# Seven-product sums made inside one PSUM bank, and the second product three steps behind instead of two

## The chip, the cores and the metric

One core of a Trainium2 chip runs the whole program. The metric is the device time of one execution in microseconds, as the median of several runs without the profiler. Engines are named as in the profile: PE is TensorE's matmuls, PEld its weight loads, DVE is VectorE, ACT is ScalarE, POOL is GpSimd, SP is SyncE, whose queue issues nearly all DMAs (SPq in the views).

## The reference

Two blocks follow each other. The first is a chunked state-space scan over 4 sequences of 8 heads, 768 positions, head size 32 and state size 16. The second is a feed-forward block on its output, read as 3072 tokens of 256 numbers:

```python
def _moe_ref(x, w_in, w_out) -> np.ndarray:
    h = x @ w_in              # 3072x256 by 256x2048
    g = h * np.cos(h)
    return (g @ w_out).astype(np.float32)   # 2048x256
```

All is float32. The scan yields, for every chunk of 32 positions, a masked product within the chunk and a product with the running state; the state decays and takes up the chunk.

## The kernel before

**Blocks and steps.** The 768 positions are cut into six blocks of 128 (`c` = 0 to 5), each with all four sequences, so that a block has 512 tokens. The scan of a block gives `yT[c]`, the features of its tokens with the feature index on the partitions. The feed-forward block then runs in steps `n` = 16 c + f. In block 0 a step takes one of two halves of the tokens (`u` = f % 2) and 256 columns of the hidden layer (`j` = f // 2); in later blocks `u` = f // 8 and `j` = f % 8. So a unit (c, u) of 256 tokens is summed over eight steps.

**One step.** `first(n)` makes `hp[n]`, 256 hidden columns by 256 tokens, in one PSUM bank (512 numbers a partition): four matmuls 128x256, eight records in the trace. Then `wind_k(n)` on ACT rounds hp/2pi to a whole number `k`, `wind_w(n)` on DVE takes the rest `w`, `gate(n)` on ACT makes the cosine, and `gated(n)` on DVE multiplies it with hp into `gT[n]`, which frees the bank. `second(n)` multiplies gT with `w_out` and adds to the unit's sums `o`. In the loop, `second(n - LAG)` stands behind `first(n)` on PE; LAG is 2.

**Seven products for eight.** From block 1 on, `seven(n)` makes the second product by Strassen's scheme in Winograd's form: a 2x2 block product in seven 128x128x128 products (14 records) in place of eight. `differ(n)` on POOL makes four differences `gd[n]` of the blocks of gT (three instructions; a ring of three buffers), `differ_w` those of the weights. The seven sums of a unit stay in two banks, `lo` and `hi`. After the unit's last step ACT copies them to `ps`, DVE or POOL adds them up into `sum`, and SP stores that. In block 0 the copy is called `ob`.

**Seven products in the first product too.** The steps in `runs` (f = 10 to 12 of blocks 2 to 4, and the thirteen steps 81 to 93) make `hp` by the same scheme in `first7`. Product 1 goes to quarter 0 of the hp bank, products 6, 7, 5 and 4 to two more banks (`at6`, `at`, from a pair called m), 3 and 2 to hp. ACT copies quarter 0 to SBUF (`parts`), and DVE makes four sums (lines 773, 776, 778 and 781). `first_of_seven(n)` writes the order out by hand: products 1 and 6 of step n, the copy, `wind_k(n - 1)`, the other five products, then `wind_w(n - 1)`, the sums, `gate(n - 1)` and `gated(n - 1)`; the seven products of `second(n - LAG)` follow on PE in one piece.

**Banks.** PSUM has eight: two of tag h (hp), two of tag o (the sums), and two pairs of tag scan. In the runs hp takes turns between the two of tag h and one half of a pair, so a step's hp bank was that of step n - 3; outside the runs hp has the two of tag h, and `first(n)` waits for `gated(n - 2)`.

**Order of work.** The order on every engine is the order in which the code issues; a wait stops all that stands behind it on its engine. At the start, `first_steps` sets out steps 0 to 3, between which DVE, ACT and POOL unpack the weights (`grade`, `join`; each 512 KB piece of `w_in` and `w_out` comes as 8-byte words). The loop starts at n = 4 (`AHEAD`), where no `second` stands:

```python
        if n == AHEAD + 1:
            second(AHEAD - LAG)
        if n >= LAG and n != AHEAD:
            second(n - LAG)
```

The scan of block 2 and later works on `blocks`, loaded by SP in groups of two issues (`load_blocks`, lines 147 and 150), transposed by DVE (line 582), scaled by ACT to `cT` (line 591), and multiplied on PE by `inner2` (line 603), for block 2 behind the `second` of step 24.

Of the kernel before, what the change touches and what calls it, by code (L numbers as in the profile page):

```python
# [10 lines left out]
I32 = mybir.dt.int32  # L11
AF = mybir.ActivationFunctionType
ALU = mybir.AluOpType
# [12 lines left out]
def kernel(  # L26
# [23 lines left out]
    HH = H // 2  # L50
    RB = 96
    NU = NB * H * NC // RB
    LAG = 2
    W = P // 2

    const = ctx.enter_context(tc.tile_pool(name="const", bufs=1))
# [606 lines left out]
                between()  # L663

    def wind_k(n):
        k = ffn.tile([P, TB], I32, tag="k", name="k")
        ACT.activation(k, hp[n], AF.Copy, bias=0.25, scale=INV_2PI)  # L667
        turns[n] = k

# [47 lines left out]


    win4 = w_in.rearrange("p k (j e f) -> p k j e f", j=NJ, e=2)
    wid, yd = [], {}  # L720

    def differ_in(i, js):

# [18 lines left out]
        eng.tensor_tensor(out=d[:, i, us], in0=a_, in1=b_,  # L742
                          op=ALU.add if i in (1, 2) else ALU.subtract)

    def first7(n, to_, at6, at, between):

        c, f = divmod(n, NF)
        u, j = turn_of(n)
        hp[n] = to_
        to_ = to_.rearrange("p (q m) -> p q m", q=4)  # L750
        w = {1: win4[:, 0, j, 0], 2: win4[:, 1, j, 0], 3: wid[3][:, j], 4: win4[:, 1, j, 1],
             5: wid[0][:, j], 6: wid[2][:, j], 7: wid[1][:, j]}
        d, y = yd[c][:, :, u], yT[c][:, u].rearrange("p k (h i) -> p k h i", h=2)
        y_ = {1: y[:, 0, 0], 2: y[:, 1, 0], 3: y[:, 1, 1], 4: d[:, 3], 5: d[:, 0], 6: d[:, 2],
              7: d[:, 1]}
        dst = {6: at6, 1: to_[:, 0], 7: at[:, 0], 5: at[:, 1], 4: at[:, 2], 3: to_[:, 1],
               2: to_[:, 0]}

        def product(q):
            PE.matmul(dst[q], lhsT=w[q], rhs=y_[q], start=(q in (6, 1, 7)), stop=True,  # L760
                      skip_group_check=True)

        parts = ms[3].rearrange("p (t q m) -> p t q m", t=2, q=4)[:, n % 2]
        add = dict(op=ALU.add)
        for q in (1, 6):
            product(q)
        ACT.copy(out=parts[:, 0], in_=to_[:, 0])
        between()
        while finished:
            finished.pop()()  # L770
        for q in (7, 5, 4, 3, 2):
            product(q)
        V.tensor_tensor(out=parts[:, 1], in0=at6, in1=parts[:, 0], **add)

        def rest():
            V.tensor_tensor(out=parts[:, 2:4], in0=at[:, 0:2],
                            in1=parts[:, 1:2].to_broadcast([P, 2, P]), **add)
            V.tensor_tensor(out=to_[:, 2:4], in0=at[:, 2:0:-1],
                            in1=parts[:, 2:3].to_broadcast([P, 2, P]), **add)

        return rest, lambda: V.tensor_tensor(out=to_[:, 1], in0=to_[:, 1], in1=parts[:, 3], **add)

    unit_rows = out.rearrange("(s q k i) m -> q k i s m", s=2, q=2, i=W)

    def second(n):
        c, f = divmod(n, NF)
        if c > 0:
            seven(n)
            return
        u, j = turn_of(n)  # L790
        if j == 0:
            o[c, u] = bank([P, 2, DM], "o", "o")
        g = gT.pop(n)
        for e in range(2):
            for t in range(2):
                PE.matmul(o[c, u][:, t], lhsT=g[:, 2 * e + t], rhs=w_out[:, 2 * j + e],  # L796
                          start=(j == e == t == 0), stop=(j == NJ - 1 and e == 1),
                          skip_group_check=True)
        if j < NJ - 1:
            return  # L800
        ob = conv.tile([P, 2, DM], FP32, tag="last", bufs=3, name="ob")
        ACT.copy(out=ob, in_=o[c, u])
        for p in range(2):
            nc.sync.dma_start(out=unit_rows[p, u], in_=ob[p * W:(p + 1) * W])

    def seven(n):

        c = n // NF
        u, j = turn_of(n)
        final = n >= NC * NF - NJ  # L810
        if j == 0:


            if final:
                t = pair("o").rearrange("p b (q m) -> p b q m", m=P)
                mid, hi = t[:, 0], t[:, 1]
                lo = bank([P, 4, P], "o", "o")
                o[c, u] = (mid, lo, hi, {1: mid[:, 0], 6: mid[:, 1], 7: mid[:, 2], 5: mid[:, 3],
                                         2: lo[:, 0], 3: lo[:, 1], 4: hi[:, 0]})
            else:  # L820
                lo, hi = (bank([P, 4, P], "o", "o") for _ in range(2))
                o[c, u] = (lo, hi, {1: lo[:, 0], 6: lo[:, 1], 2: lo[:, 2], 7: hi[:, 0],
                                    5: hi[:, 1], 4: hi[:, 2], 3: hi[:, 3]})
        at = o[c, u][-1]
        g = gT.pop(n)
        if n == NC * NF - 1:
            last_step(g, *o[c, u][1:3])
            return
        d = gd.pop(n)
        w = {1: w4[:, j, 0, 0], 2: w4[:, j, 1, 0], 3: w4[:, j, 1, 1], 4: wd[3][:, j],  # L830
             5: wd[0][:, j], 6: wd[2][:, j], 7: wd[1][:, j]}
        a_ = {1: g[:, 0], 2: g[:, 2], 3: d[:, 3], 4: g[:, 3], 5: d[:, 0], 6: d[:, 2], 7: d[:, 1]}
        starts = (1, 2, 4) if final else (1, 7)
        for q in ((1, 4, 7, 5, 6, 2, 3) if final else (1, 2, 7, 5, 6, 4, 3) if n in sevens else
                  (1, 2, 6, 7, 5, 4, 3)):
            PE.matmul(at[q], lhsT=a_[q], rhs=w[q], start=(j == 0 and q in starts),  # L836
                      stop=(j == NJ - 1), skip_group_check=True)
        if final and j == NJ - 2:
            shared(o[c, u][0])
        if j < NJ - 1:  # L840
            return

        sum_ = two.tile([P, 7, P], FP32, tag="sum", bufs=1, name="sum")
        ps = two.tile([P, 7, P], FP32, tag="ps", bufs=1, name="ps")
        lo, hi = o[c, u][0:2]

        def take():
            ACT.copy(out=ps[:, 0:3], in_=lo[:, 0:3])
            ACT.copy(out=ps[:, 3:7], in_=hi)

        if n + LAG + 1 in sevens:
            finished.append(take)
        else:
            take()

        def rest(of=range(4), eng=V):
            for dst, a_, b_ in [((sum_[:, 0:2], ps[:, 1:3], ps[:, 0:1]),
                                 (sum_[:, 5:7], ps[:, 3:5], sum_[:, 0:1]),
                                 (sum_[:, 3:5], ps[:, 5:3:-1], sum_[:, 5:6]),
                                 (sum_[:, 2:3], ps[:, 6:7], sum_[:, 6:7]))[i] for i in of]:  # L860
                eng.tensor_tensor(out=dst, in0=a_, in1=b_.to_broadcast([P, dst.shape[1], P]),
                                  op=ALU.add)
            for s in range(2 if 3 in of else 0):
                nc.sync.dma_start(out=unit_rows[s, 2 * c + u], in_=sum_[s * W:(s + 1) * W, 1:5].rearrange(
                                      "p (t h) m -> p t (h m)", t=2))

        unsummed.append(rest)
# [156 lines left out]
    runs = [*(range(NF * c + 10, NF * c + 13) for c in range(2, NC - 1)),  # L1024
            range(NC * NF - 15, NC * NF - 2)]
    sevens = {n: r for r in runs for n in r}
    late, at_ = [], {}

    def first_of_seven(n):

        i = n - sevens.get(n, sevens.get(n - 1))[0]
        if i == 0:
            at_["hp"] = pair("hp")[:, 0]
            at_["m"] = pair("m").rearrange("p b (q m) -> p b q m", m=P)
        if n == NC * NF - NJ + LAG + 1:
            at_["hp"] = bank([P, TB], "hp", "o")
        to_ = at_["hp"] if i % 3 == 1 else bank([P, TB], "hp", "h")
        if n not in sevens:
            first(n, to_=to_)
            return  # L1040
        sums, last_sum = first7(n, to_, at_["m"][:, 1, 0], at_["m"][:, 0],
                                lambda: wind_k(n - 1) if i else None)
        if i:
            wind_w(late[0])
        sums()
        gate(late[0]) if i else None
        gated(late.pop())
        last_sum()

    def first_steps():  # L1050

# [52 lines left out]
    for n in range(AHEAD, NC * NF + LAG):  # L1104
        c, f = divmod(n, NF)
        if n < NC * NF:
# [10 lines left out]
                load_along(2, (2 * (n == NF), 2 * (n == NF) + 1))  # L1117
            for e, i in chunks_at(n, "along"):
                load_along(e + 1, (2 * i, 2 * i + 1))
            if n in sevens or n - 1 in sevens:  # L1120
                first_of_seven(n)
            else:
                first(n)
            if n not in sevens and n - 1 in sevens:
                wind(n - 1)
                gate(n - 1)
                gated(late.pop())
            closing = f == NF - 1 and 1 <= c < NC - 1
            take_y = finish2(c + 1) if closing else None
            if n not in sevens:  # L1130
# [29 lines left out]
            behind = [lambda k=k: weights(k, 1) for k in units_at(n - 1, 3)] + behind  # L1160
            if not joins and behind:
                behind.pop(0)()
            if n + 1 in sevens or n in sevens:
                late.append(n)
            else:
                gated(n)
            if closing:
                take_y(1)
# [28 lines left out]
        for start, js in zip((2 * NF - 5, 3 * NF - 3, 4 * NF - 3),  # L1197
                             (slice(2, 5), slice(0, 2), slice(5, NJ))):
            if start <= n < start + 4:
                differ_in(n - start, js)  # L1200
        if n == AHEAD + 1:
            second(AHEAD - LAG)
        if n >= LAG and n != AHEAD:
            second(n - LAG)
        for e, _ in chunks_at(n, "inner"):
            inner2(e)
        for k in units_at(n, 3):
# [49 lines left out]
```

## Time and profile before

| | us |
|---|---|
| median of 3 runs | 364.75 (364.12 to 365.27) |
| profiled execution: span from first to last instruction (the page gives no other time of it) | 369.8 |
| PE busy | 359.4 |
| PEld busy | 327.8 |
| DVE busy | 270.8 |
| POOL busy | 233.0 |
| ACT busy | 182.3 |

| group | count | mean ns of one |
|---|---|---|
| PE hp, 128x256 (line 660) | 592 | 386 |
| PE 128x128 products (lines 760, 836) | 308 and 1106 | 275 to 278 |
| ACT k, line 667 | 96 | 595 |
| ACT cosine, line 682 | 96 | 723 |
| DVE w, line 673 | 96 | 685 |
| DVE gT, line 687 | 96 | 682 |
| DVE sums of hp, lines 773, 776, 778, 781 | 22 each | 291, 415, 433, 289 |
| ACT copy of quarter 0, line 767 | 22 | 262 |
| ACT copies `lo`, `hi`, lines 848, 849 | 9 each | 471, 596 |
| ACT copy 128x256 (yT, line 636) | 16 | 379 |

A record's duration contains time in which the next one already runs, so that matmuls are costed by the distance between starts: 0.112 us for a 128x128 record and 0.216 for a 128x256 one in this trace. A float32 matmul leaves two records. The span lies above the median, so that the profiled execution is slower than the others; differences are worked out within the profile.

### The profile page before, as it was taken

How to read it: one execution, taken by the hardware profiler on the slowest of the kernel's cores; microseconds unless marked ns; L12 is line 12 of the kernel's file. 1: busy time of each engine (PE TensorE's matmuls, PEld its weight loads, DVE VectorE, ACT ScalarE, POOL GpSimd, SP SyncE). 2: the span in 40 equal slices, each digit the busy share in tenths (PEclk: the TensorE clock that was granted, in tenths of full speed). 3: DMA queues.
4: the chain of work that ended last, by engine and by line, in shares of the span. 5: the costliest groups of instructions: out<-in, count | busy, mean ns of one | idle time of the engine just before them, and what ended most of it. 6: DMA issues, size and time to landing. Idle time of an engine off the chain costs nothing.

```text
span 369.8 us, 10169 instructions
## 1 busy us (share of the span) xinstructions
PE 359.4 (97%) x4034; PEld 327.8 (89%) x4034; DVE 270.8 (73%) x492; ACT 182.3 (49%) x346; POOL 233.0 (63%) x375
## 2 busy tenths in 40 slices
PE   8999999999959999999999999999999999999995
PEld 5688888898948989999999999999999999999995
DVE  7699988588735794887757788756796565688874
ACT  4588756463433435453545453445553444455542
POOL 6567656679816676466676656679556465375572
PEclk9999999999996999999999999999999999999999
DMA  7996855593566416344005441001010001001002
GB/s 141 259 361 133 186 119 92 82 151 64 125 100 90 88 44 98 52 79 82 13 4 110 59 79 37 6 4 42 2 30 0 2 2 31 2 2 29 2 10 51
DMA packets 97328, 26.43 MB, mean 71 GB/s; under 512 B 87328, under 2 KB 93184, under 8 KB 97280
## 3 DMA queue, kind: packets, MB, share of 16 engines
q1 hardware_dynamic: 96032, 25.38, 33.7%
q8 instruction: 32, 0.52, 0.6%
q10 hardware_dynamic: 1248, 0.39, 0.5%
q14 instruction: 16, 0.13, 0.1%
HBM read 22.36 MB, written 3.34 MB: 69 GB/s over the span
## 4 chain that ended last, share of the span: by engine, by line
PE 83%; DVE 4%; POOL 3%; ACT 2%; DMA 2%; SPq 2%; issue 2%; DVEq 0%; ACTq 0%; POOLq 0%
PE o L836 31%; PE hp L660 30%; PE m L760 5%; PE o L796 5%; PE hp L760 4%; PE y L629 2%; PE g L603 1%; DMA blocks<-in_C_dram 1%; SPq L150 1%; POOL gd L712 1%; DVE mag L261 1%; DMA bc<-in_B_dram 1%; POOL gd L714 1%; DVE w L673 1%; PE y L617 1%
## 5 line engine op out<-in xcount | busy, mean ns | idle before, releaser
L660 PE MATMUL hp<-yT,w_in 128*128 128x256 f32 x592 | 143.0, 386 | 0.4 <-DVE gT L687 0.4
L660 PEld LDWEIGHTS hp<-yT,w_in 128*128 128x128 f32 x592 | 108.8, 192 | 15.6 <-issue 1.6
L712 POOL TENSOR_TENSOR gd<-gT 128x256 f32<-128x256 f32 x79 | 59.8, 758 | 89.4 <-DVE gT L687 74.3
L682 ACT ACTIVATE w<-w,quarter 128x512 f32<-128x512 f32 x96 | 69.4, 723 | 68.1 <-DVE w L673 68.0
L673 DVE SCALAR_TENSOR_TENSOR w<-hp,k 128x512 f32<-128x512 f32 x96 | 65.8, 685 | 50.3 <-ACT k L667 50.0
L667 ACT ACTIVATE k<-hp 128x512 int32<-128x512 f32 x96 | 57.1, 595 | 77.8 <-PE hp L660 70.4
L687 DVE TENSOR_TENSOR gT<-hp,w 128x512 f32<-128x512 f32 x96 | 65.5, 682 | 17.2 <-ACT w L682 12.5
L836 PE MATMUL o<-words,gd 128*128 128x128 f32 x474 | 66.1, 276 | 0.1
L836 PEld LDWEIGHTS o<-words,gd 128*128 128x128 f32 x474 | 59.4, 192 | 0.3 <-POOL gd L714 0.3
L836 PE MATMUL o<-w_out,gT 128*128 128x128 f32 x316 | 50.1, 278 | 0.0
L836 PEld LDWEIGHTS o<-w_out,gT 128*128 128x128 f32 x316 | 46.6, 193 | 3.2
L714 POOL TENSOR_TENSOR gd<-gT,gd 128x128 f32<-128x128 f32 x79 | 40.4, 512 | 6.2
L715 POOL TENSOR_TENSOR gd<-gT,gd 128x128 f32<-128x128 f32 x79 | 39.0, 494 | 6.2
L836 PE MATMUL o<-w_out,gd 128*128 128x128 f32 x158 | 30.7, 276 | 0.0
L836 PE MATMUL o<-words,gT 128*128 128x128 f32 x158 | 30.6, 275 | 0.0
L796 PE MATMUL o<-w_out,gT 128*128 128x256 f32 x128 | 29.9, 379 | 0.0
L375 DVE TENSOR_TENSOR_SCAN lam<-arow,unit 128x512 f32<-128x512 f32 x20 | 29.8, 1489 | 0.0
L796 PEld LDWEIGHTS o<-w_out,gT 128*128 128x128 f32 x128 | 24.3, 190 | 3.2
L836 PEld LDWEIGHTS o<-words,gT 128*128 128x128 f32 x158 | 24.0, 192 | 0.0
L836 PEld LDWEIGHTS o<-w_out,gd 128*128 128x128 f32 x158 | 24.0, 192 | 0.0
L760 PE MATMUL m<-m,wid 128*128 128x128 f32 x132 | 18.3, 275 | 0.0
L760 PE MATMUL hp<-yT,w_in 128*128 128x128 f32 x88 | 17.0, 275 | 0.0
(130 smaller groups left out, 429.9 us busy)
## 6 DMA issues: line engine op xcount, KB each, us to landing
words<-in_moe_w_in_dram SPq DMA_DIRECT2D x8, 512.0 KB
words<-in_moe_w_out_dram SPq DMA_DIRECT2D x8, 512.0 KB
xr<-in_x_dram SPq DMA_DIRECT2D x24, 128.0 KB
arow<-a_cut SPq DMA_DIRECT2D x10, 256.0 KB
arow<-a_cut SPq DMA_DIRECT2D x10, 252.0 KB
out_dram<-sum SPq DMA_DIRECT2D x18, 128.0 KB
bc<-in_B_dram SPq DMA_DIRECT2D x24, 64.0 KB
blocks<-in_B_dram SPq DMA_DIRECT2D x16, 32.0 KB
```

Source lines behind the costliest of these rows:

```text
L375: V.tensor_tensor_scan(out=lams[k][:, p, hs].rearrange(flat), data0=rows_.rearrange(flat), data1=unit0[:, hs].rearrange(flat), initial=0.0 ...
L660: PE.matmul(to_[:, e], lhsT=w_in[:, k, fs], rhs=y[:, k], start=(k == 0), stop=(k == KT - 1), skip_group_check=True)
L667: ACT.activation(k, hp[n], AF.Copy, bias=0.25, scale=INV_2PI)
L673: V.scalar_tensor_tensor(out=w, in0=hp[n], scalar=INV_2PI, in1=k, op0=ALU.mult, op1=ALU.subtract)
L682: ACT.activation(cos, cos, AF.Sin, bias=quarter, scale=TWO_PI)
L687: V.tensor_tensor(out=gT[n], in0=hp.pop(n), in1=cos, op=ALU.mult)
L712: G.tensor_tensor(out=d[:, 0:2], in0=g[:, 1:2].to_broadcast([P, 2, P]), in1=g[:, 3::-3], op=ALU.subtract)
L714: G.tensor_tensor(out=d[:, 2], in0=g[:, 0], in1=d[:, 0], op=ALU.subtract)
L715: G.tensor_tensor(out=d[:, 3], in0=g[:, 2], in1=d[:, 2], op=ALU.subtract)
L760: PE.matmul(dst[q], lhsT=w[q], rhs=y_[q], start=(q in (6, 1, 7)), stop=True, skip_group_check=True)
L796: PE.matmul(o[c, u][:, t], lhsT=g[:, 2 * e + t], rhs=w_out[:, 2 * j + e], start=(j == e == t == 0), stop=(j == NJ - 1 and e == 1), skip_gr ...
L836: PE.matmul(at[q], lhsT=a_[q], rhs=w[q], start=(j == 0 and q in starts), stop=(j == NJ - 1), skip_group_check=True)
```

## The change

`LAG` becomes 3, with rings to match: gT has LAG + 1 buffers, four for three, and the ring of `k` goes from three to two. At the start `second` now stands behind every step from n = 5 on, one each.

In the seven-product steps, all seven products of hp go to the hp bank itself, in three groups. `begin7` makes products 1, 5 and 7 in quarters 1, 0 and 2; ACT copies 7 and 5 to `parts` and product 1 into quarter 0. Products 6 and 2 are then added by TensorE onto quarters 1 and 0. Two DVE instructions write quarters 2 and 1 (with 7 and 5 from `parts`) and quarter 3. Products 3 and 4 are added by TensorE onto quarters 1 and 2, in the next step. `period7` writes the order of a step out, with `second(n - LAG)` cut in three pieces between the groups. When a unit ends there, `end7` has ACT copy `lo` at once and `hi` in the next step. The bank pair m is not used any more.

```diff
--- before.py
+++ after.py
@@ -50,7 +50,7 @@
     HH = H // 2
     RB = 96
     NU = NB * H * NC // RB
-    LAG = 2
+    LAG = 3
     W = P // 2
 
     const = ctx.enter_context(tc.tile_pool(name="const", bufs=1))
@@ -663,7 +663,7 @@
                 between()
 
     def wind_k(n):
-        k = ffn.tile([P, TB], I32, tag="k", name="k")
+        k = ffn.tile([P, TB], I32, tag="k", bufs=2, name="k")
         ACT.activation(k, hp[n], AF.Copy, bias=0.25, scale=INV_2PI)
         turns[n] = k
 
@@ -717,7 +717,7 @@
 
 
     win4 = w_in.rearrange("p k (j e f) -> p k j e f", j=NJ, e=2)
-    wid, yd = [], {}
+    wid, yd, rest7 = [], {}, {}
 
     def differ_in(i, js):
 
@@ -742,50 +742,44 @@
         eng.tensor_tensor(out=d[:, i, us], in0=a_, in1=b_,
                           op=ALU.add if i in (1, 2) else ALU.subtract)
 
-    def first7(n, to_, at6, at, between):
+    def begin7(n, to_):
 
         c, f = divmod(n, NF)
         u, j = turn_of(n)
         hp[n] = to_
-        to_ = to_.rearrange("p (q m) -> p q m", q=4)
+        at = to_.rearrange("p (q m) -> p q m", q=4)
         w = {1: win4[:, 0, j, 0], 2: win4[:, 1, j, 0], 3: wid[3][:, j], 4: win4[:, 1, j, 1],
              5: wid[0][:, j], 6: wid[2][:, j], 7: wid[1][:, j]}
         d, y = yd[c][:, :, u], yT[c][:, u].rearrange("p k (h i) -> p k h i", h=2)
         y_ = {1: y[:, 0, 0], 2: y[:, 1, 0], 3: y[:, 1, 1], 4: d[:, 3], 5: d[:, 0], 6: d[:, 2],
               7: d[:, 1]}
-        dst = {6: at6, 1: to_[:, 0], 7: at[:, 0], 5: at[:, 1], 4: at[:, 2], 3: to_[:, 1],
-               2: to_[:, 0]}
-
-        def product(q):
-            PE.matmul(dst[q], lhsT=w[q], rhs=y_[q], start=(q in (6, 1, 7)), stop=True,
-                      skip_group_check=True)
-
-        parts = ms[3].rearrange("p (t q m) -> p t q m", t=2, q=4)[:, n % 2]
-        add = dict(op=ALU.add)
-        for q in (1, 6):
-            product(q)
-        ACT.copy(out=parts[:, 0], in_=to_[:, 0])
-        between()
-        while finished:
-            finished.pop()()
-        for q in (7, 5, 4, 3, 2):
-            product(q)
-        V.tensor_tensor(out=parts[:, 1], in0=at6, in1=parts[:, 0], **add)
-
-        def rest():
-            V.tensor_tensor(out=parts[:, 2:4], in0=at[:, 0:2],
-                            in1=parts[:, 1:2].to_broadcast([P, 2, P]), **add)
-            V.tensor_tensor(out=to_[:, 2:4], in0=at[:, 2:0:-1],
-                            in1=parts[:, 2:3].to_broadcast([P, 2, P]), **add)
-
-        return rest, lambda: V.tensor_tensor(out=to_[:, 1], in0=to_[:, 1], in1=parts[:, 3], **add)
+        parts = ms[3].rearrange("p (t q m) -> p t q m", t=4, q=2)[:, n % 2]
+
+        def products(*of):
+            for q, i in of:
+                PE.matmul(at[:, i], lhsT=w[q], rhs=y_[q], start=(q == 1), stop=True,
+                          skip_group_check=True)
+
+        def copies():
+            ACT.copy(out=parts, in_=at[:, 2::-2])
+            ACT.copy(out=at[:, 0], in_=at[:, 1])
+
+        def sums():
+            V.tensor_tensor(out=at[:, 2:0:-1], in0=at[:, 1:2].to_broadcast([P, 2, P]),
+                            in1=parts, op=ALU.add)
+            V.tensor_tensor(out=at[:, 3], in0=at[:, 1], in1=parts[:, 0], op=ALU.add)
+
+        products((1, 1), (5, 0), (7, 2))
+        copies()
+        rest7[n] = (lambda: products((6, 1), (2, 0)), sums, lambda: products((3, 1), (4, 2)))
 
     unit_rows = out.rearrange("(s q k i) m -> q k i s m", s=2, q=2, i=W)
 
     def second(n):
         c, f = divmod(n, NF)
         if c > 0:
-            seven(n)
+            for part in seven(n):
+                part()
             return
         u, j = turn_of(n)
         if j == 0:
@@ -825,16 +819,25 @@
         g = gT.pop(n)
         if n == NC * NF - 1:
             last_step(g, *o[c, u][1:3])
-            return
+            return ()
         d = gd.pop(n)
         w = {1: w4[:, j, 0, 0], 2: w4[:, j, 1, 0], 3: w4[:, j, 1, 1], 4: wd[3][:, j],
              5: wd[0][:, j], 6: wd[2][:, j], 7: wd[1][:, j]}
         a_ = {1: g[:, 0], 2: g[:, 2], 3: d[:, 3], 4: g[:, 3], 5: d[:, 0], 6: d[:, 2], 7: d[:, 1]}
         starts = (1, 2, 4) if final else (1, 7)
-        for q in ((1, 4, 7, 5, 6, 2, 3) if final else (1, 2, 7, 5, 6, 4, 3) if n in sevens else
-                  (1, 2, 6, 7, 5, 4, 3)):
-            PE.matmul(at[q], lhsT=a_[q], rhs=w[q], start=(j == 0 and q in starts),
-                      stop=(j == NJ - 1), skip_group_check=True)
+
+        def products(*of):
+            for q in of:
+                PE.matmul(at[q], lhsT=a_[q], rhs=w[q], start=(j == 0 and q in starts),
+                          stop=(j == NJ - 1), skip_group_check=True)
+
+        order = (1, 4, 7, 5, 6, 2, 3) if final else (1, 2, 6, 7, 5, 4, 3)
+        cut = 3 if j == 0 and not final else 4
+        return (lambda: products(*order[:2]), lambda: products(*order[2:cut]),
+                lambda: (products(*order[cut:]), end7(n, c, u, j, final)))
+
+    def end7(n, c, u, j, final):
+
         if final and j == NJ - 2:
             shared(o[c, u][0])
         if j < NJ - 1:
@@ -843,9 +846,9 @@
         sum_ = two.tile([P, 7, P], FP32, tag="sum", bufs=1, name="sum")
         ps = two.tile([P, 7, P], FP32, tag="ps", bufs=1, name="ps")
         lo, hi = o[c, u][0:2]
+        ACT.copy(out=ps[:, 0:3], in_=lo[:, 0:3])
 
         def take():
-            ACT.copy(out=ps[:, 0:3], in_=lo[:, 0:3])
             ACT.copy(out=ps[:, 3:7], in_=hi)
 
         if n + LAG + 1 in sevens:
@@ -1024,28 +1027,39 @@
     runs = [*(range(NF * c + 10, NF * c + 13) for c in range(2, NC - 1)),
             range(NC * NF - 15, NC * NF - 2)]
     sevens = {n: r for r in runs for n in r}
-    late, at_ = [], {}
-
-    def first_of_seven(n):
+    at_ = {}
+
+    def bank_of(n):
 
         i = n - sevens.get(n, sevens.get(n - 1))[0]
         if i == 0:
             at_["hp"] = pair("hp")[:, 0]
-            at_["m"] = pair("m").rearrange("p b (q m) -> p b q m", m=P)
-        if n == NC * NF - NJ + LAG + 1:
-            at_["hp"] = bank([P, TB], "hp", "o")
-        to_ = at_["hp"] if i % 3 == 1 else bank([P, TB], "hp", "h")
-        if n not in sevens:
-            first(n, to_=to_)
-            return
-        sums, last_sum = first7(n, to_, at_["m"][:, 1, 0], at_["m"][:, 0],
-                                lambda: wind_k(n - 1) if i else None)
-        if i:
-            wind_w(late[0])
-        sums()
-        gate(late[0]) if i else None
-        gated(late.pop())
-        last_sum()
+        return at_["hp"] if i % 3 == 1 else bank([P, TB], "hp", "h")
+
+    def gates(n):
+        wind(n)
+        gate(n)
+        gated(n)
+
+    def period7(n):
+
+        begin7(n, bank_of(n))
+        while finished:
+            finished.pop()()
+        first_, then, last_ = seven(n - LAG)
+        first_()
+        if n - 1 in sevens:
+            rest7[n - 1][2]()
+            wind_k(n - 1)
+        then()
+        rest7[n][0]()
+        if n - 1 in sevens:
+            wind_w(n - 1)
+        rest7[n][1]()
+        if n - 1 in sevens:
+            gate(n - 1)
+            gated(n - 1)
+        return last_
 
     def first_steps():
 
@@ -1117,14 +1131,14 @@
                 load_along(2, (2 * (n == NF), 2 * (n == NF) + 1))
             for e, i in chunks_at(n, "along"):
                 load_along(e + 1, (2 * i, 2 * i + 1))
-            if n in sevens or n - 1 in sevens:
-                first_of_seven(n)
+            second_ = lambda n=n: second(n - LAG)
+            if n in sevens:
+                second_ = period7(n)
+            elif n - 1 in sevens:
+                first(n, rest7[n - 1][2], to_=bank_of(n))
+                gates(n - 1)
             else:
                 first(n)
-            if n not in sevens and n - 1 in sevens:
-                wind(n - 1)
-                gate(n - 1)
-                gated(late.pop())
             closing = f == NF - 1 and 1 <= c < NC - 1
             take_y = finish2(c + 1) if closing else None
             if n not in sevens:
@@ -1160,9 +1174,7 @@
             behind = [lambda k=k: weights(k, 1) for k in units_at(n - 1, 3)] + behind
             if not joins and behind:
                 behind.pop(0)()
-            if n + 1 in sevens or n in sevens:
-                late.append(n)
-            else:
+            if n not in sevens:
                 gated(n)
             if closing:
                 take_y(1)
@@ -1198,10 +1210,10 @@
                              (slice(2, 5), slice(0, 2), slice(5, NJ))):
             if start <= n < start + 4:
                 differ_in(n - start, js)
-        if n == AHEAD + 1:
-            second(AHEAD - LAG)
-        if n >= LAG and n != AHEAD:
+        if n >= NC * NF:
             second(n - LAG)
+        elif n > AHEAD:
+            second_()
         for e, _ in chunks_at(n, "inner"):
             inner2(e)
         for k in units_at(n, 3):
```

## The prediction

> **What bounds the kernel now.** I read the page first (busy times and slices), then the busy times by stage, the waits of TensorE, and the timelines of the three places that the change touches.
>
> ```profile
> PE 359.4 (97%) x4034; PEld 327.8 (89%) x4034; DVE 270.8 (73%) x492; ACT 182.3 (49%) x346; POOL 233.0 (63%) x375
> ...
> PE   8999999999959999999999999999999999999995
> ```
>
> ```profile
> 34.00:106.00 72.00, 71.85 (x706) 63.34 (x706) 56.35 (x83) 40.42 (x76) 50.51 (x62) 1.00 0.65 122
> 106.00:117.00 11.00, 6.78 (x78) 5.37 (x78) 4.28 (x6) 2.04 (x4) 6.14 (x11) 0.69 0.63 94
> 117.00:176.00 59.00, 59.00 (x687) 54.75 (x687) 45.89 (x80) 26.74 (x50) 35.58 (x60) 1.00 0.41 73
> ...
> 316.00:356.00 40.00, 40.00 (x358) 39.90 (x357) 31.75 (x76) 20.56 (x40) 24.21 (x43) 1.00 0.04 8
> ```
>
> The columns are the stage, its length, then busy time of PE, PEld, DVE, ACT and POOL, granted clock, DMA share and GB/s. TensorE has no free time from 34 to 106 and from 117 on; VectorE is at 31.75 of 40 us even in the long run of seven-product steps (316 to 356). Busy TensorE could still hide short stalls, so I looked at its pace: in the run below one step begins at 327.61 and the next at 330.74, 3.13 us for 28 records of 128x128, 0.224 us a product (two records), and a plain pair of steps takes 1.73 + 1.56. It runs at its pace. So taking work from VectorE can give nothing in these stages; what counts is what makes TensorE wait. Today that is little:
>
> ```profile
> PE g L603 <- ACT cT L591: 4.2, 1, 4.2
> ...
> PE hp L660 <- DVE gT L687: 0.4, 1, 0.4
> ```
>
> **The change, part by part.** My sum is made against the profiled execution, span 369.8 us, which is 5.05 us above the median of 364.75 us; I add the difference to the median.
>
> *One more step of lag.* No product is added, so TensorE's work is the same; `second(n)` moves one step back in its queue. In the first steps before, `second(2)` and `second(3)` stand together after `first(5)`; after, `second(3)` stands behind `first(6)`. What `first(6)` needs is a bank, hp(4), freed by gT(4) on VectorE:
>
> ```profile
> 30.04 3.62 PE L796 MATMUL o<-w_out,gT 128*128 128x256 f32 x16
> 33.19 0.68 DVE L687 TENSOR_TENSOR gT<-hp,w 128x512 f32<-128x512 f32 x1
> 34.01 1.97 PE L660 MATMUL hp<-yT,w_in 128*128 128x256 f32 x8 [0.35 <-DVE gT L687]
> 35.82 1.89 PE L796 MATMUL o<-w_out,gT 128*128 128x256 f32 x8
> ```
>
> The 16 records at 30.04 are `second(2)` and `second(3)`; VectorE works without a break on joins, w and gT up to 33.87, and none of it depends on `second(3)`. So `first(6)` still starts at 34.0, and TensorE stands still from 31.8 to 34.0: the 1.73 us of `second(3)` are no longer done under that wait. From 34 on each `first` starts as before with a `second` one number lower behind it, TensorE is full, and the owed step is paid at the end: +1.73, or +1.56 where the wait at 106 swallows the 0.17 by which `second(15)` (plain) is longer than `second(16)` in its slot. I take +1.6. Bounds: nothing, if VectorE is earlier in unprofiled executions, and 1.73.
>
> The row that bears on the clock is the 4.2 us wait below, after which the records run at half pace; 2.2 us of standing still has no row. The Trainium skill (TensorE: Matmul & The Clock Gate, "What's actually happening") puts the fall to half clock after an idle window of about 3.4 us; by it the new wait leaves the clock alone, and if it did not, about 3 us more would be lost, an estimate from the rows below.
>
> The lag also moves the copy `ob`, its two output pairs on SP, the copies `ps` and the sums of `second`. On SP the output pairs pass behind other issues, in front of the last C blocks on which the 4.2 us wait hangs:
>
> ```profile
> 103.34 1.40 SPq L150 DMA_DIRECT2D blocks<-in_C_dram  x2
> ...
> 109.17 0.63 DVE L582 STREAM_TRANSPOSE turned<-blocks 128x256 f32<-128x256 f32 x1 [4.43 <-DMA blocks<-in_C_dram]
> ...
> 110.80 1.99 PE L603 MATMUL g<-cT,turned 32*64 32x128 f32 x56 [4.22 <-ACT cT L591]
> ```
>
> SP issues without a break from 84 to 114 us. Both output pairs stay ahead of this C pair and `ob` is written by 80 us, about 83 after the change, before SP comes to it at 92. Same issues ahead, so I count 0; the swapped pairs last 1.36 and 1.26, so it may be 1.3 us either way. Later output pairs are waited for by no engine.
>
> At the end, `second(94)` and the last step wait little for gd and gT now (0.15 + 0.1 us of uneven record starts near 363.3 and 364.0); with three steps of cover that goes: -0.25 (bounds 0 and -0.3). Deeper rings (gT 4, k 2) remove no wait that a row shows; k(n) needs w(n-2) done, a step earlier.
>
> *The seven products of hp* (22 steps). Four VectorE sums (291 + 415 + 433 + 289 = 1428 ns) become two (433 + 289 by the nearest rows, 722): VectorE loses 15.5 us, worth nothing while TensorE is full. ScalarE has two copies (379 + 262 ns) for one (262): +8.3 us beside TensorE. The new waits are those of products 6 and 2 for the copies, and of 3 and 4 for the sums. What stands behind a waiting product is all of TensorE. I set them out on the rows of one step:
>
> ```profile
> 327.61 0.39 PE L760 MATMUL hp<-yT,w_in 128*128 128x128 f32 x2
> 328.09 0.27 ACT L767 COPY m<-hp 128x128 f32<-128x128 f32 x1 [0.57 <-PE hp L760]
> 328.55 0.60 ACT L667 ACTIVATE k<-hp 128x512 int32<-128x512 f32 x1 [0.19 <-DVE hp L781]
> 329.21 0.68 DVE L673 SCALAR_TENSOR_TENSOR w<-hp,k 128x512 f32<-128x512 f32 x1
> 329.92 0.72 ACT L682 ACTIVATE w<-w,quarter 128x512 f32<-128x512 f32 x1 [0.77 <-DVE w L673]
> 330.32 0.43 DVE L778 TENSOR_TENSOR hp<-m 128x256 f32<-128x256 f32 x1
> 330.74 0.39 PE L760 MATMUL hp<-yT,w_in 128*128 128x128 f32 x2
> ```
>
> Handovers read from it: TensorE's last record ends 0.17 after its pitch, PE to ACT 0.1, k to w 0.06, w to gate 0.03, DVE to PE 0.1 (33.87 to 34.01 above). With product 1 of step n at 0, the order is 1,5,7 (to 0.67), two of `second`, 3 and 4 of step n-1 (1.12 to 1.56), two of `second`, 6 and 2 (2.01 to 2.45), three of `second` (to 3.13).
> Copies: product 7 ends 0.84, ACT 0.94 to 1.58, free for TensorE 1.68; wanted at 2.01: 0.3 to spare.
> Sums: 4 of n-1 ends 1.73, k 1.83 to 2.43, w 2.49 to 3.17, sums to 3.90, TensorE 4.0; wanted at 3.13 + 1.12 = 4.25: 0.25 to spare. This is the loop from step to step, about 2.9 us in a period of 3.13.
> At the end of a run product 3 stands behind half a plain `first`: wanted at 3.13 + 0.87 = 4.0, nothing to spare: 0.05 each, four runs, 0.2.
> Where a unit ends, the next `second` needs the bank that the `lo` copy (471 ns) empties, and its first two products now stand 0.67 into the step. In the runs of blocks 2 to 4 this falls in their second step: last product ends 3.30, copy 3.40 to 3.87, TensorE 3.97, wanted at 3.80: 0.17 each, 0.5 together. In the last run the copy stands behind gate(n-1) on ACT (3.21 to 3.93), ends about 4.32, TensorE 4.42 against 3.80: 0.6.
> Sum 0.2 + 0.5 + 0.6 = 1.3. Bounds: 0, if handovers are as short as the shortest seen, and 0.2 in each of 22 steps, 4.4, if the loop misses its period by a little.
>
> A rule speaks against summing in one bank: PSUM — Partial Sum Buffer, "PSUM bank collisions raise a hardware error", wants every access of another engine to a bank kept apart from TensorE's by a semaphore. Alone, an estimate by it puts copies and sums bare in TensorE's way, some 1.7 us a step, 37 us; by the rows products on other banks fill both gaps.
>
> **Sum:** +1.6 - 0.25 + 0 + 1.3 = +2.65: span 372.4, median 367.4.
>
> **Rivals.** *The loop does not fit.* For it: 0.25 to spare over five handovers, and VectorE's other work can come between. Then every seven-product step pays 0.2 or more: 4.4 in place of 1.3, 370.5; decisive from 3.13 us for the loop. *The owed step is free.* If without the profiler gT(4) lands by 31.9 rather than 33.87, `first(6)` is not held and the lag costs nothing; with waits of 1.3 at most, less 0.25, it ends at 364.5 to 365.8, not slower by what can be measured. For it: the 5.05 us that profiling adds lie somewhere; against it: VectorE has no break in that stretch. *The wait at 106 shrinks.* After that wait the records to 117 run at half pace: 1.91 for 56 records (later 1.14 for 63), 3.58 for a `first` (1.73), 0.80 for four records (0.45): 3.1 us. If SP's new order brings the C blocks 1.3 us earlier and the clock stays up, 2.65 - 1.3 - 3.1 = -1.75: 363.0. The order of issues gives no reason for that.
>
> **How the numbers follow.** A measurement here can tell about 0.3%, 1.1 us, from no change. Forecast 0.61, loop 0.18, free step 0.13, shorter wait 0.08. Slower 0.79, same 0.13, faster 0.08. The range takes the forecast with its unknowns (0.3 to 4.4 for the runs), the loop case and most of the free step: 365.0 to 370.7.
>
> **What would show it.** Right: TensorE waits about 2.1 us for gT before the matmul at 34.0; the wait of L603 stays near 4.2; in 3 + 1 places a product of `second` waits for ACT; DVE busy near 255 us. Wrong: DVE's gT frees hp(4) earlier; waits of products 3 or 6 in every step; a C block landing more than 1 us from 109.

## The result and the profile after

The changed kernel takes 367.79 us, the median of four executions (366.60 to 368.03), beside 364.44 us for the kernel before on the same chip: a ratio of 1.0091, 95% interval 1.0068 to 1.0115, which is 3.35 us more. The forecast was 367.4. The sign, the main cause and nearly the size are as predicted, but part of the closeness is luck: a term that was left out and terms that were rated too high nearly balanced each other. This is worked out below.

The profile page of the changed kernel, busy times and slices:

```profile
PE 356.8 (98%) x4034; PEld 326.0 (89%) x4034; DVE 259.0 (71%) x448; ACT 191.6 (53%) x368; POOL 234.1 (64%) x375
...
PE   8997999999999999999999999999999999999995
...
PEclk9999999999999999999999999999999999999999
```

VectorE lost 11.8 us (270.8 before) and ScalarE gained 9.3 (182.3), and TensorE has the same 4034 records. The slice that was a 5 before (102 to 111 us) is a 9 now; a 7 has come in the fourth slice, 27 to 36 us. The granted clock is 9, which is 90% or more, in every slice. The same stages by window (length, then busy time of PE, PEld, DVE, ACT, POOL, granted clock, DMA share, GB/s):

```profile
34.00:106.00 72.00, 71.65 (x700) 63.39 (x700) 58.18 (x87) 41.30 (x79) 51.26 (x64) 1.00 0.67 122
106.00:117.00 11.00, 11.00 (x130) 10.09 (x129) 8.44 (x13) 5.06 (x9) 9.02 (x16) 1.00 0.64 93
...
316.00:356.00 40.00, 40.00 (x346) 39.58 (x345) 25.50 (x49) 24.51 (x50) 25.94 (x47) 1.00 0.03 8
```

In the long run of seven-product steps VectorE fell from 31.75 (30.79 in the repeated execution of the kernel before) to 25.50 of 40 us, and TensorE is as full as it was: the relief buys nothing there. The stage at 106 is full and at full clock, where the profile before had 6.78 of 11 us. That is no gain of the change, as the first repeated run will show.

What TensorE waits for in the changed kernel (total, times, longest):

```profile
PE hp L660 <- DVE gT L687: 2.1, 1, 2.1
...
PE o L831 <- ACT ps L849: 0.3, 1, 0.3
```

Both waits were forecast; three more of the second kind, in the short runs, were forecast and did not come. The first in its place on the timeline:

```profile
30.38 1.89 PE L790 MATMUL o<-w_out,gT 128*128 128x256 f32 x8
...
34.35 1.97 PE L660 MATMUL hp<-yT,w_in 128*128 128x256 f32 x8 [2.08 <-DVE gT L687]
36.15 1.89 PE L790 MATMUL o<-w_out,gT 128*128 128x256 f32 x8
```

Where 16 records of two `second`s stood before `first(6)`, eight stand now, and the matmul that needs gT(4) still starts at 34.35. VectorE, which delivers it, is no earlier. The time of the missing `second` has become waiting.

### The profile page after: what moved, and what is told of

It reads as the page before. It is cut to its first block, busy times and chain, and to the rows that moved or that the text cites. A ratio compares the mean times of both kernels' runs of the same rounds, so it can differ in the third digit from the quotient of the medians.

```text
span 364.7 us, 10134 instructions
## 1 busy us (share of the span) xinstructions
PE 356.8 (98%) x4034; PEld 326.0 (89%) x4034; DVE 259.0 (71%) x448; ACT 191.6 (53%) x368; POOL 234.1 (64%) x375
## 4 chain that ended last, share of the span: by engine, by line
PE 95%; DVE 2%; ACT 1%; issue 1%; ACTq 0%; DVEq 0%
PE hp L660 35%; PE o L831 34%; PE hp L760 9%; PE o L790 7%; PE y L629 2%; PE g L603 1%; PE y L477 1%; PE y L617 1%; PE g L456 1%; PE a_ps L364 1%; PE warm L84 1%; PE y L525 1%; PE y L515 1%; PE o L891 0%; DVE mag L261 0%
## 5 line engine op out<-in xcount | busy, mean ns | idle before, releaser
L660 PEld LDWEIGHTS hp<-yT,w_in 128*128 128x128 f32 x592 | 107.5, 190 | 16.4 <-POOL mag L249 2.5
L831 PE MATMUL o<-words,gd 128*128 128x128 f32 x474 | 69.4, 275 | 0.0
L831 PEld LDWEIGHTS o<-words,gd 128*128 128x128 f32 x474 | 61.0, 192 | 0.0
L375 DVE TENSOR_TENSOR_SCAN lam<-arow,unit 128x512 f32<-128x512 f32 x20 | 29.0, 1448 | 0.0
L760 PE MATMUL hp<-m,wid 128*128 128x128 f32 x132 | 22.3, 278 | 0.0
L760 PEld LDWEIGHTS hp<-m,wid 128*128 128x128 f32 x132 | 18.2, 192 | 0.2
```

Of the source, the lines that this page charges most:

```text
L375: V.tensor_tensor_scan(out=lams[k][:, p, hs].rearrange(flat), data0=rows_.rearrange(flat), data1=unit0[:, hs].rearrange(flat), initial=0.0 ...
L660: PE.matmul(to_[:, e], lhsT=w_in[:, k, fs], rhs=y[:, k], start=(k == 0), stop=(k == KT - 1), skip_group_check=True)
L760: PE.matmul(at[:, i], lhsT=w[q], rhs=y_[q], start=(q == 1), stop=True, skip_group_check=True)
```

## The experiments

The theory, A: the time is lost by the lag, whose third step is taken up where TensorE has nothing else to do, plus short waits where runs and units end; the three groups themselves fit into the step. Rivals: B, the lag costs nothing and the groups cost the time; and for the size, that the clock falls in the new wait.

**The two kernels again, as they are (`before_again`, `after_again`, and on another chip `after_third`).** Nothing is edited.

> The kernel before, unchanged, profiled once more. Theory A, the 4.2 us wait at 106 us and the half-pace records after it belong to that one execution: the span is about 362.3 us (369.8 less the wait of 4.4 and 3.1 of half pace), TensorE waits for no C block, and the first matmul of step 6 still waits 0.35 us at 34. Rival B, the wait is part of every execution before the change and the change takes it away: the span is again near 369.8 with a wait of about 4 us at 106.

> The changed kernel, unchanged, timed in more rounds to narrow the difference. From the two traces without the wait at 106 I work out +1.73 at step 6, about +0.5 in the three short runs, +0.46 at step 83 and -0.25 at the end: +2.4 us over before, 366.9 us. The first timing said +3.35. If the sum of the traces is complete the difference comes out at 2.4, if something is missing from it it stays at 3 or more. Profile: a wait of about 2.1 us for gT at 34 again.

> The changed kernel, profiled a third time. If the clock falls at 35 again the device time is near 368.2 or above, if it stays up near 366.6; a time near 368 with the clock up speaks against the clock as the cause of the spread.

The kernel before took 364.38 us with a span of 362.6 us. TensorE's waits in it begin with these three, all of the first 9 us, and `L603` is not among them; later it waits once for gT, 0.4 us:

```profile
PE warm L84 <- PEq L1241: 0.8, 1, 0.8
PE tp L409 <- DMA bc<-in_B_dram: 0.7, 1, 0.7
PE g L456 <- ACT cT L399: 0.5, 1, 0.5
...
PE hp L660 <- DVE gT L687: 0.4, 1, 0.4
```

So the 4.2 us wait for the C blocks and the half pace after it belonged to the one execution that I had read, and the median never held them. The device time lies 364.38 - 362.6 = 1.8 us above the span, and 366.60 - 364.7 = 1.9 in the changed kernel. The 5.05 us between the first span and the median was not what profiling adds but that wait.

The changed kernel gave 368.44 us in six executions against 364.88, a ratio of 1.0091 (1.0068 to 1.0114), and 366.48 in the one on the other chip. So the +2.4 us that the two traces gave was not all of the difference. The span in `after_again` is 367.7, 3.0 us over the first profile's 364.7. One microsecond of that is a later start (a DMA of the first 9 us); for the rest, this is the place of the new wait, and the window around it:

```profile
31.47 1.89 PE L790 MATMUL o<-w_out,gT 128*128 128x256 f32 x8
35.44 3.65 PE L660 MATMUL hp<-yT,w_in 128*128 128x256 f32 x8 [2.08 <-DVE gT L687]
```

```profile
35.00:39.00 4.00, 3.56 (x9) 2.88 (x10) 3.26 (x5) 2.10 (x4) 3.31 (x4) 0.57 1.00 196
```

The eight records of `first(6)` take 3.65 us instead of 1.97, at a granted clock of 0.57 over the 4 us. The clock's own records in this trace put it at half from 35.54 to 38.95, 3.41 us. The wait is no longer than in the first profile, 2.08 us in both, where the clock stayed up. Each execution carries its mean granted clock, and they fall into two groups: eight of the eleven of the changed kernel stand at 0.994 or 0.995 (367.69 to 369.57 us), three at 0.999 or 1.0 (366.48, 366.60 and 368.12; why the last is late was not seen, it has no profile). Half clock for 3.41 us of 366 makes 1 - 0.5 x 3.41 / 366 = 0.995, which is the lower group. All 35 executions of the kernel before that ran beside these stand at 0.998 or above.

**The lag alone, at the start (`e1_lag3_start`).** The kernel before, with three steps of lag in block 0 and the rings for it; at n = 16 the owed `second` is caught up. The seven-product steps are those of before.

```diff
-        k = ffn.tile([P, TB], I32, tag="k", name="k")
+        k = ffn.tile([P, TB], I32, tag="k", bufs=2, name="k")
...
-        gT[n] = ffn.tile([P, TB], FP32, tag="gT", bufs=LAG + 1, name="gT")
+        gT[n] = ffn.tile([P, TB], FP32, tag="gT", bufs=LAG + 2, name="gT")
...
-        if n == AHEAD + 1:
-            second(AHEAD - LAG)
-        if n >= LAG and n != AHEAD:
-            second(n - LAG)
+        if n == NF:
+            second(n - LAG - 1)
+        if n > AHEAD:
+            second(n - LAG - (1 if n < NF else 0))
```

> The kernel before with the lag of three in block 0 alone: second(3) stands behind first(6), and step 16 makes up for it with two seconds; seven-product steps as before. Theory A, the owed step: TensorE waits about 2.1 us at 34 instead of 0.35 and the 1.73 us are not regained, 366.2 us. Rival B, the cost of the change lies in the seven-product steps and the lag is free: 364.4 us.

366.77 us, ratio 1.0055 (1.0035 to 1.0076), 2.0 us more, with this at the start:

```profile
30.92 1.89 PE L796 MATMUL o<-w_out,gT 128*128 128x256 f32 x8
34.88 1.97 PE L660 MATMUL hp<-yT,w_in 128*128 128x256 f32 x8 [2.07 <-DVE gT L687]
```

The wait comes with the lag and without the groups. Of seven executions, two have a mean clock of 0.995 and take 367.81 us, and one takes 367.90 at full clock, which nothing here explains. The four others lie at 366.45 to 366.77, 1.6 to 1.9 above 364.88: the 1.73 us of one plain `second`. That is the 366.2 of A as nearly as the scatter allows, and not the 364.4 of B.

**The groups, with the lag taken up later (`e2_late_lag`).** The changed kernel, with lag 2 to n = 28, no `second` at n = 29, and lag 3 from 30 on, where the scan of a block gives TensorE other work.

```diff
+    TURN = NF + 13
...
+        if n == AHEAD + 1:
+            second(AHEAD - 2)
         if n >= NC * NF:
             second(n - LAG)
-        elif n > AHEAD:
+        elif n > AHEAD and n < TURN:
+            second(n - 2)
+        elif n > TURN:
             second_()
```

> The changed kernel with the lag of two until step 28, no second in step 29 and the lag of three from step 30 on: there the 1.6 us of open2 stand behind the first matmuls, and the bank that step 30 needs should be free by then. Theory A, the owed step: the wait at 34 is 0.35 us, TensorE does not stand still at step 30, and the time is 1.7 us under the changed kernel, about 366.1 us. Rival B: no change, 367.8 us. If step 30 has to wait for its bank, the gain is smaller by that wait, which the profile shows.

365.50 us in twelve executions, ratio 1.0009 (0.9993 to 1.0026); against `after_again`, on the same chip, 2.9 us less. The wait at 34 is 0.3 us as before, and the place where the `second` is left out now looks like this:

```profile
120.96 1.89 PE L660 MATMUL hp<-yT,w_in 128*128 128x256 f32 x8
122.78 0.91 PE L617 MATMUL y<-rT,state 32*64 32x64 f32 x64
...
124.41 1.99 PE L660 MATMUL hp<-yT,w_in 128*128 128x256 f32 x8
```

`first(30)` starts without a wait: the products of the scan between the two steps give VectorE the time that the `second` gave. The gain is more than the 1.7 that A expected, since the drop of the clock goes with the wait (no execution below 0.998). B falls: most of the cost is in where the lag is taken up. What is left to the groups is under 1 us (spans of 363.5 and 362.6).

**The groups with two steps of lag (`e3_groups_lag2`).** The changed kernel with the lag of before.

```diff
-    LAG = 3
+    LAG = 2
...
+        if n == AHEAD + 1:
+            second(AHEAD - LAG)
```

> The changed kernel with a lag of two everywhere: the products of hp in three groups as in the change, but second(n - 2) cut between them. Theory A, the groups need the third step: the differences gd of step n - 2 come from POOL 1.77 us after gT, which is itself only ready 4.7 us after the start of its step, so the second piece of second(n - 2), wanted at 1.56 of the next step, waits 1.3 us or more in each of 22 steps, and its first piece for gT 0.9: 367.9 - 1.7 + 22 x 1.4 = about 397 us. Rival B, the lag is not needed and only costs the step at 34: 366 us.

381.92 us, ratio 1.0471 (1.0447 to 1.0494). Neither number was right; A's was 15 us too high. One step of the long run:

```profile
333.06 0.39 PE L760 MATMUL hp<-yT,w_in 128*128 128x128 f32 x2
...
334.11 0.71 PE L831 MATMUL o<-w_out,gT 128*128 128x128 f32 x4 [0.22 <-DVE gT L687]
...
335.51 0.71 PE L831 MATMUL o<-words,gd 128*128 128x128 f32 x4 [0.24 <-POOL gd L714]
...
337.18 0.39 PE L760 MATMUL hp<-yT,w_in 128*128 128x128 f32 x2
```

The step takes 337.18 - 333.06 = 4.12 us instead of 3.13. VectorE's gT(n - 2) runs from 333.36 to 334.05, 1.0 us into step n, and `second(n - 2)` wants it at 0.67; POOL's differences come as late to the next piece. So both pieces wait in this step. From the fourth step of the long run on all steps but one take as long (4.11 to 4.13 us, once 3.61), while the first two steps of a run take 3.31 and 3.13, in the long run 2.80 and 3.13. A had put 1.4 us on each of 22 steps, and that is why its number is too high. About 9.6 of the 17.4 us that this kernel loses to the one before lie in the long run, and about 2 around each short one. The groups need the third step of lag.

**The copy of `lo` ahead of the gate (`e4_late_lag_early_lo`).** `e2_late_lag`, and where a unit ends in `period7`, its last piece of `second` is issued before `gate(n - 1)`, and with it the copy of `lo`.

```diff
         rest7[n][1]()
+        if turn_of(n - LAG)[1] == NJ - 1:
+            last_()
+            last_ = lambda: None
         if n - 1 in sevens:
             gate(n - 1)
```

> The late lag (two until step 28, none at 29, three from 30), and at the end of a unit inside a run the ACT copy of the first bank of sums stands ahead of the gate instead of behind it. Theory A: the wait of a product of second for ACT in the long run falls from 0.46 to about 0.2 us, nothing else changes: about 0.3 us below the late lag alone, 365.2 us, no difference from before that can be told. Rival B: the gate that is now later delays gT and the next step's copies, and the waits come back in products 6 or 3.

364.76 us in twelve executions against 364.54, ratio 1.0003 (0.9994 to 1.0011): no difference from the kernel before that can be measured. First the unit's end in the changed kernel, then here:

```profile
313.78 0.72 ACT L682 ACTIVATE w<-w,quarter 128x512 f32<-128x512 f32 x1 [0.76 <-DVE w L673]
...
314.41 0.46 ACT L849 COPY ps<-o 128x384 f32<-128x384 f32 x1
...
314.92 0.71 PE L831 MATMUL o<-w_out,gT 128*128 128x128 f32 x4 [0.30 <-ACT ps L849]
```

```profile
311.07 0.60 ACT L667 ACTIVATE k<-hp 128x512 int32<-128x512 f32 x1 [0.24 <-PE hp L760]
311.57 0.47 ACT L849 COPY ps<-o 128x384 f32<-128x384 f32 x1
...
312.43 0.72 ACT L682 ACTIVATE w<-w,quarter 128x512 f32<-128x512 f32 x1 [0.39 <-DVE w L673]
...
313.11 0.61 PE L831 MATMUL o<-w_out,gT 128*128 128x128 f32 x4
```

In the changed kernel the copy runs behind the gate and the next `second` waits. Here it runs in front, at 311.57, while three products of the same `second` are still to come: none of them touches `lo`, which was full with the second piece. The wait is gone whole, and this step takes 3.13 us where the changed kernel's took 3.69 (from 313.79 to 317.48). In the time of the whole kernel, set against `e2_late_lag`, so little is not resolved: the spans lie 0.8 us apart (363.5 and 362.7), the ratios 0.0006, or 0.2 us, with intervals that overlap.

**Other work in the wait (`e5_filled_wait`).** The changed kernel, with a matmul of ones, two records 128x512, on a spare bank behind `second(2)`; it computes nothing that is used.

```diff
             second_()
+        if n == AHEAD + 1:
+            fill(pair("warm")[:, 0].rearrange("p (q i) -> p q i", q=4))
```

> The changed kernel with two matmul records of no use (ones by ones, 128x512, as at the start of the program) put behind second(2), into the wait of step 6: it computes the same. Theory A, the wait lowers the granted clock in those executions in which it falls inside one of the clock's periods, as in the second profile (half pace from 35.5 to 38.95, 1.7 us lost): the filling leaves a wait of about 1.3 us, the clock stays up, the fast executions stay at 366.6 and the others come down to that, median about 366.9 us against 368.2. Rival B, the spread of the runs has another cause: median unchanged at 368.2.

366.73 us, ratio 1.0061 (1.0045 to 1.0076), where the changed kernel had 1.0091 (1.0068 to 1.0114) on the other chip. The intervals overlap, so that a gain in time is not shown; it is no slower, although TensorE does more.

```profile
31.83 1.02 PE L84 MATMUL warm<-const-float32-1.0 128*128 128x512 f32 x2
34.08 1.97 PE L660 MATMUL hp<-yT,w_in 128*128 128x256 f32 x8 [1.22 <-DVE gT L687]
```

`first(6)` starts where it did, behind a wait of 1.22 us, and all six executions stand at 0.999 or 1.0. So the time of the wait stays, as idle time or as useless work, and the clock fell in none of the six. One reserve: on this chip the changed kernel was run once, and there too its clock stayed up (366.48). That the filling kept the clock up is therefore argued from the executions on the other chip, and not shown.

## Why the prediction was right, and where it was not

**The owed step, +1.6: right.** The wait rose from 0.4 to 2.1 us with gT(4) where it had been, and `e1` gives 1.6 to 1.9 for it alone. The rival that the owed step is free falls by that. In the traces it comes back where the prediction put it: from the start of the last group of scan matmuls of block 5 (301.33 and 301.50) to TensorE's last matmul it is 57.11 us in `before_again` and 58.92 in the changed kernel, of which 1.56 is the `second` of seven products that is done there.

**The clock in the new wait: the step that failed.** The prediction weighed the rule of the Trainium skill (TensorE: Matmul & The Clock Gate, "What's actually happening") and let the new wait leave the clock alone. The runs: half clock for 3.41 us in `after_again`, 0.994 or 0.995 in eight of eleven executions, none in `e2` and `e5`, which have no such wait. The term is 1.7 us in that trace (3.65 - 1.97), 1.3 between the groups of the first four executions (about 367.9 and 366.6); the prediction had 0, and named about 3 for the case that it fell. So the measurement goes against the rule as the prediction used it: 2.08 us of standing still was enough. The page also says that its window of about 3.4 us runs free, whatever the kernel does; that sentence, which I had not used, agrees with the run-to-run changes here.

**What profiling adds: a misreading.** I worked with the differences, so the forecast did not depend on what made up the 5.05 us. But the first profile held a wait of its own, and the rival that it might shrink (363.0) was built on it: in the repeated execution of before there was nothing to shrink. "The wait of L603 stays near 4.2" failed for the same reason. A C block more than 1 us from 109 us, named as a sign of being wrong, came too (its transposition starts at 104.64 in the changed kernel), but `before_again` has it at 104.65, so that this is not the change. The 0 for SP's new order held: the C pair is issued at 99.42 in `before_again` and at 99.41 in the changed kernel.

**The ends of runs and units, 1.3: nearly the size, the place wrong in part.** From the start of a block's first scan products (`L603`) to that of its next ones (`L617`), which takes in one short run, TensorE takes 27.16 us before (27.26 in one of the three) and 27.35 after: about 0.19 for each short run, where 0.22 (0.17 and 0.05) was forecast. It is not the `lo` copy: in the first run that starts at 169.89 us, and no product of the step that begins at 171.14 is late. About 0.1 is product 6 in the first step of each run. There are no products 3 and 4 of a step before, so that product 6 is wanted at 1.57 and not at 2.01; my schedule had the copies done at 1.68, but I held that against the steady step alone. In the trace the second copy ends at 1.52, and the two records of product 6 start at 1.58 and 1.79, the second 0.1 late. The other 0.08 lies in the products of `L603` ahead of the run, whose 64 starts are spread over 1.01 us instead of 0.94; why was not found. In the long run `second` starts 0.46 us late at the unit's end (forecast 0.6), by the mechanism named, the copy behind the gate; but the copy needed only the second piece of `second`, not its last product, as `e4` shows. My schedule took the last product for the release, and so missed the order that avoids the wait.

**The loop from step to step: right.** One step of the long run in the changed kernel, from product 1 of one step to product 3 in the next:

```profile
320.61 0.39 PE L760 MATMUL hp<-yT,w_in 128*128 128x128 f32 x2
...
322.37 0.60 ACT L667 ACTIVATE k<-hp 128x512 int32<-128x512 f32 x1 [0.24 <-PE hp L760]
322.62 0.39 PE L760 MATMUL hp<-m,wid 128*128 128x128 f32 x2
...
323.00 0.69 DVE L673 SCALAR_TENSOR_TENSOR w<-hp,k 128x512 f32<-128x512 f32 x1 [0.52 <-ACT k L667]
...
323.61 0.42 DVE L768 TENSOR_TENSOR hp<-hp,m 128x256 f32<-128x256 f32 x1
...
323.74 0.39 PE L760 MATMUL hp<-yT,w_in 128*128 128x128 f32 x2
...
324.07 0.30 DVE L770 TENSOR_TENSOR hp<-hp,m 128x128 f32<-128x128 f32 x1
...
324.85 0.39 PE L760 MATMUL hp<-yT,wid 128*128 128x128 f32 x2
```

The step takes 323.74 - 320.61 = 3.13 us, as before. Product 6 starts at 2.01 (wanted at 2.01), product 3 at 4.24 (wanted at 4.25), and the sums end at 3.76, where I had 3.90. So the rival that the loop does not fit falls. At this pace no product of the step waits for the bank that TensorE shares with the other engines.

**The small terms.** The 0.25 of the end measures 0.21: three starts near 356 us come 0.04, 0.09 and 0.09 late in `before_again`, and none in the changed kernel. "Deeper rings remove no wait that a row shows" held, but the third step of lag removes one that the sum did not have: `before_again` has starts that are 0.26 and 0.10 late at 88.9 us, in the third seven-product `second`, where it takes up its differences. The changed kernel has none; `e2`, with the deeper rings but a lag of two at this place, still has them (0.28 and 0.10). VectorE is at 259.0, not near 255. The records of the sums did lose the 15.5 us (31.4 before, 15.9 after); but neighbouring records overlap, by 25.0 us in all before and 21.5 after, and busy time counts that time once, so that only 11.8 of it shows. It decides nothing.

**The sum by the traces,** from `first(6)` to the last matmul, with the clock up: -0.32 to the scan of block 2, +0.57 from there to that of block 5 (the short runs), +1.81 at the end (1.56 + 0.46 - 0.21; the other small differences of the long run cancel), together +2.06; the spans differ by 364.7 - 362.6 = 2.1. The prediction had 2.65. What carries the median to 3.35 is the clock in most of the executions. The -0.32 holds +0.17, by which the `second` that has come into this stretch is longer, and -0.36 of the uneven starts above; the rest was not traced. So the forecast came close by luck as well as by its mechanism: a term that was left out (about 1.3 in most executions) was offset by the others, rated 0.6 too high together.

## What to carry to other kernels

A deeper pipeline does not add work, but where it is entered it takes one step out of the queue, and that step is free only where something else fills the place: take the delay up beside other work that the engine has, as `e2` does, and not where the first steps already wait. Relieving an engine that is not the bound is worth nothing by itself: 11.8 us of VectorE became 0 in `e4`, the version without the other costs. Read two executions before a wait is taken for the kernel's: of the one stall that the first profile showed, the second showed nothing.

## What the runs showed of the hardware

A wait of 2.1 us was enough to halve TensorE's clock, for one stretch of 3.41 us, and not in every execution of the same kernel. The clock's records in the traces are multiples of 3.41 us long. Counted in such periods, the wait of `after_again` fell wholly into one (32.13 to 35.54, 2.08 us idle), and the clock dropped for the next. In the first profile of the changed kernel a boundary at 33.21 split it into 0.93 and 1.14; in `e1` 1.74 fell into one period; in `after_third` 1.84 did, from 32.58 on. In these three the clock stayed up, as here in `after_third`, where eight records take 1.97 us behind a wait as long:

```profile
34.41 1.97 PE L660 MATMUL hp<-yT,w_in 128*128 128x256 f32 x8 [2.07 <-DVE gT L687]
```

An estimate from these four rows is that between 1.84 and 2.08 us of idle time in one period is the limit. A wait of 2.08 us that falls by chance would then lower the clock in 39 to 53% of the executions (an estimate too); 10 of 18 stand at 0.994 or 0.995 (8 of 11 of the changed kernel, 2 of 7 of `e1`). It is four traces, and no run moved the wait against the period on purpose, so that the limit itself is argued and not shown; measured is that with the wait filled down to 1.22 us the clock stayed up in all six executions.
